# Dealing out the output matmuls of a fused attention and feed-forward kernel in pairs, with the routing of a batch's first pair moved forward in its stretch

## The chip, the cores and the metric

The kernel runs on one core of one Trainium2 chip. The metric is the device time of one execution in microseconds. Every comparison is made with runs of the kernel before on the same chip in the same rounds. "Lost" time below is TensorE's: the length of a stretch less the work in it, counted as instructions times the cadence at which TensorE issues them when nothing waits (the prediction tells where the cadences come from).

## The reference

Clustered attention, then a feed-forward layer with `h * cos(h)` in the middle. There are 4 batches, 8 heads, 768 positions, head size 64; then 3072 tokens, model width 512, inner width 2048.

```
q_assign = argmax(q_n @ c_n.T);  k_assign = argmax(k_n @ c_n.T)       # routing: 16 clusters a head
mask     = q_assign[:, :, :, None] == k_assign[:, :, None, :]
attn     = softmax(where(mask, q @ k.T / 8, -1e9))
x        = (attn @ v) laid out as (tokens, 512)
h        = x @ w_in
out      = (h * cos(h)) @ w_out
```

## The kernel before

Heads are taken two at a time: 16 pairs, four to a batch. The program is a row of **pair stretches**, one per pair, with an **input stage** after the stretches of each batch. A pair stretch has nine score chunks as its main work. Each chunk goes through an exponential on ScalarE:

```
def e_chunk(p, c):
    ps = ps_big.tile([P, CW], FP32, name="big")          # two such PSUM buffers, 1024 columns each
    ...  # 2 or 3 matmuls from the transposed q and k, with the routing as 16 more rows (L332)
    nc.scalar.activation(out=e_flat[...], in_=ps, func=AF.Exp, scale=1.0 / SUNIT)
```

Other work is strewn between the chunks as filling:

```
f_list(p)       # attention times V, 12 times 6 matmuls (L352), then normalization on DVE (L362, L363)
g_list(p)       # transpose of the result into xt: by DMA, or for a batch's last pair by TensorE (L378)
tr_list(p)      # halving of q and k into high and low fp16 parts on DVE (L198, L200), transpose by DMA (L234)
c_list(p)       # routing: 4 times 6 matmuls (L250), then reductions on DVE
ot_list(p)      # transpose of the routing by DMA (L286), four copies of it into qkT (L290)
moe2_list(b, t) # one output tile: 8 items of two matmuls (L416), then a copy on DVE (L421) and a store
```

`merge` spreads a list of filling evenly over the main work by weight. The order on ScalarE and GpSimd is the program's. TensorE, DVE and the DMA queue are put in order by the compiler, which may lift an instruction ahead of its place. At run time an engine takes its instructions in the order it got: in the traces below, DVE stands for 2.50 us and TensorE for 4.15 us at an instruction whose input has not come, with others behind it.

The input stage of a batch is 12 chunks of 16 matmuls (L394), with a cosine on ScalarE (L401) and a product on DVE (L402). A batch has six output tiles. Two are made in its input stage; four are left for the next batch's pair stretches:

```
for s in range(NPE - 1, NPAIR):
    late = s % HPB == 2
    fill = []
    if not late: fill += cs("E", s)              # routing
    fill += trs("E", s)                          # halvings and transposes
    after_s = s > HPB and s % HPB == 1           # the first pair after an input stage
    if not after_s: fill += f_list(s - 1) + g_list(s - 1)
    if m2:                                       # whole output tiles, 16 matmuls each
        left = HPB - (s - 1) % HPB
        keep = 2 if s + HPB >= NPAIR else 0
        for _ in range(-(-max(0, len(m2) - keep) // left)):
            fill += moe2_list(*m2.pop(0))
    if late: fill += cs("E", s)                  # routing of pair s + 2, a batch's first, comes last
    ...
```

In the last stage, TensorE has the last pair's L352, then 12 input chunks, with all the output tiles that are left as filling.

The softmax here doesn't subtract the row's maximum and nothing guards it: scores larger than these inputs give would overflow.

## Time and profile before

The median is 318.27 us of three runs (317.21 to 318.49). The first pairs go another way through the program, and the change doesn't touch them, so the table begins at stretch 5. It is worked out from the timeline of PE.

| part | begins at, us | length, us | lost, us |
|---|---|---|---|
| stretches 5 / 6 / 7 / 8 | 91.40 | 9.28 / 9.65 / 10.91 / 10.24 | 0.57 / 0.27 / 1.38 / 0.38 |
| input stage of batch 1 | 131.48 | 31.70 | 0.44 |
| stretches 9 / 10 / 11 / 12 | 163.18 | 9.34 / 9.65 / 11.34 / 8.19 | 0.63 / 0.27 / 1.81 / 1.73 |
| input stage of batch 2 | 201.70 | 31.85 | 0.65 |
| stretches 13 / 14 | 233.55 | 9.34 / 9.33 | 0.63 / 0.56 |
| stretch 15 and the last stage, to the last tile | 252.22 | 57.41 | 0.21 |

A stretch runs from its first score matmul to the next part's first matmul, so a wait at the head of stretch 8 is counted as lost in stretch 7. Stretch 12 is short since it has no output matmul.

### The profile page before, as it was taken

Reading aid. Unit: us, or ns where it says so; the run is one execution under the profiler, and the core shown is the slowest. Engines: PE = TensorE matmul, PEld = TensorE weight load, DVE = VectorE, ACT = ScalarE, POOL = GpSimd, SP = SyncE. Lnnn points to the kernel's source line nnn. Section 1 sums busy time; section 2 is a strip of 40 time slices with the busy share of each in tenths; the row PEclk is TensorE's granted clock in tenths of the full one; section 3 lists DMA queues with packets and bytes.
Section 4 is the critical chain, followed back from the end, with each engine's and each line's share of the span. In section 5 each row is a group of like instructions: output and inputs, shape, how many; then the busy total and the mean of one; then the engine's idle time right before and its main releaser. Section 6 shows DMA issues by size and latency. Waiting matters only on the chain.

```text
span 316.7 us, 8195 instructions
## 1 busy us (share of the span) xinstructions
PE 305.7 (97%) x3459; PEld 214.8 (68%) x3459; DVE 189.3 (60%) x363; ACT 215.8 (68%) x235; POOL 75.0 (24%) x130
## 2 busy tenths in 40 slices
PE   7999999999999998999999997999999999999995
PEld 2668777887766665688766664787766566766754
DVE  4888887779966245179966145279962114355431
ACT  5688989865469897856569897865479992442220
POOL 2799945120130422220130422220020400000000
PEclk9999999999999999999999999999999999999999
DMA  6579999667597969737596999838482940000012
GB/s 203 201 131 180 234 120 140 165 149 160 88 223 134 147 134 155 195 91 156 83 233 133 145 131 139 205 87 158 94 156 73 74 62 33 35 33 35 33 52 84
DMA packets 87845, 40.25 MB, mean 127 GB/s; under 512 B 76352, under 2 KB 82752, under 8 KB 87808
## 3 DMA queue, kind: packets, MB, share of 16 engines
q1 hardware_dynamic: 57504, 24.19, 34.3%
q0 software_dynamic: 30016, 15.21, 32.4%
q8 instruction: 27, 0.44, 0.6%
q10 hardware_dynamic: 288, 0.33, 0.4%
q14 instruction: 10, 0.08, 0.1%
HBM read 27.30 MB, written 6.29 MB: 106 GB/s over the span
## 4 chain that ended last, share of the span: by engine, by line
PE 83%; ACT 8%; DVE 4%; DMA 4%; issue 1%; SPq 0%; ACTq 0%
PE big L394 25%; PE one L416 22%; PE big L332 17%; PE one L352 10%; ACT e_ring L339 6%; DMA qkT<-ohT 3%; PE one L250 2%; PE one L247 2%; PE one L306 2%; PE one L218 1%; DVE g L402 1%; DMA qk_nat<-in_q_dram 1%; PE one L433 1%; PE one L378 1%; ACT cos_t L401 1%
## 5 line engine op out<-in xcount | busy, mean ns | idle before, releaser
L339 ACT ACTIVATE e_ring<-big 128x1024 f16<-128x1024 f32 x144 | 137.7, 1037 | 16.8 <-PE big L332 15.9
L401 ACT ACTIVATE cos_t<-big,bias_pi 128x1024 f16<-128x1024 f32 x48 | 53.4, 1112 | 68.9 <-PE big L394 68.8
L416 PE MATMUL one<-w_out_sb,g 128*128 128x512 f16 x368 | 93.6, 379 | 0.0
L394 PE MATMUL big<-xt,w_in_sb 128*128 128x256 f16 x768 | 91.4, 273 | 1.0 <-DVE g L402 1.0
L332 PE MATMUL big<-qkT 128*128 128x512 f16 (+1 forms) x384 | 85.4, 325 | 3.7 <-DMA qkT<-ohT 2.6
L394 PEld LDWEIGHTS <-w_in_sb 128*128 128x128 f16 x768 | 74.0, 98 | 16.0 <-DVE g L402 1.8
L402 DVE TENSOR_TENSOR g<-big,cos_t 128x1024 f16<-128x1024 f32 x48 | 58.6, 1222 | 41.4 <-ACT cos_t L401 41.4
L416 PEld LDWEIGHTS <-g 128*128 128x128 f16 x368 | 35.0, 98 | 30.3
L332 PEld LDWEIGHTS <-qkT 128*128 128x128 f16 x384 | 33.3, 97 | 28.2 <-issue 3.7
L352 PEld LDWEIGHTS <-e_ring 128*128 128x128 f16 x1152 | 44.7, 97 | 7.7
L352 PE MATMUL one<-v_ext,e_ring 128*128 128x65 f16 x1152 | 47.2, 193 | 0.0
L421 DVE COPY o_sb<-one 128x512 f32<-128x512 f32 x23 | 15.8, 686 | 30.4 <-PE one L416 30.4
L200 DVE SCALAR_TENSOR_TENSOR stg<-qk_nat,stg 128x384 f16<-128x384 f32 x64 | 33.3, 552 | 0.2
L134 POOL DMA_DIRECT2D v_ext<-in_v_dram x32 | 26.5, 833 | 4.8 <-issue 3.1
L117 POOL COPY pace<-e_ring 1x1 f16<-1x1 f16 x30 | 5.4, 180 | 77.2 <-ACT e_ring L339 77.0
L362 DVE RECIPROCAL recip<-one 128x6 f32<-128x6 f32 x32 | 6.1, 193 | 28.2 <-PE one L352 28.1
L196 POOL TENSOR_SCALAR stg<-qk_nat 128x384 f16<-128x384 f32 x16 | 19.9, 1245 | 8.2 <-DMA qk_nat<-in_q_dram 7.0
L117 POOL COPY pace<-g 1x1 f16<-1x1 f16 x13 | 2.3, 177 | 78.2 <-DVE g L402 63.8
L363 DVE TENSOR_TENSOR av_stage<-one,recip 128x384 f16<-128x384 f32 x32 | 17.7, 557 | 1.0
L194 ACT ACTIVATE stg<-qk_nat 128x384 f16<-128x384 f32 x28 | 13.1, 513 | 2.0 <-DMA qk_nat<-in_q_dram 2.0
L318 DVE TENSOR_SCALAR qkT<-one 16x768 f16<-16x768 f16 (+1 forms) x20 | 10.9, 544 | 3.5 <-PE one L306 2.9
L198 DVE TENSOR_SCALAR stg<-qk_nat 128x384 f16<-128x384 f32 x20 | 6.8, 364 | 8.8 <-DMA qk_nat<-in_q_dram 6.0
(57 smaller groups left out, 168.1 us busy)
## 6 DMA issues: line engine op xcount, KB each, us to landing
out_dram<-o_sb SPq DMA_DIRECT2D x23, 256.0 KB, 2.3
qk_nat<-in_q_dram POOLq DMA_DIRECT2D x10, 384.0 KB, 3.7
qk_nat<-in_k_dram POOLq DMA_DIRECT2D x10, 384.0 KB, 4.1
v_ext<-in_v_dram POOLq DMA_DIRECT2D x32, 96.0 KB, 4.0
w_in_sb<-in_moe_w_in_dram POOLq DMA_DIRECT2D x4, 512.0 KB, 7.1
w_out_sb<-in_moe_w_out_dram POOLq DMA_DIRECT2D x4, 512.0 KB, 6.6
qk_nat<-in_q_dram SPq DMA_DIRECT2D x5, 384.0 KB, 6.5
qk_nat<-in_k_dram SPq DMA_DIRECT2D x5, 384.0 KB, 7.1
```

The source lines that it names most:

```text
L134: nc.gpsimd.dma_start(out=v_bufs[p % NV][:, hh, :, 0:D], in_=v[b, 2 * hp + hh].rearrange("(p t) d -> p t d", p=P))
L196: nc.gpsimd.tensor_scalar_mul(dst[:, :, 0, :], src, ASCALE)
L200: nc.vector.scalar_tensor_tensor(out=dst[:, :, 1, :], in0=src, scalar=ASCALE, in1=dst[:, :, 0, :], op0=ALU.mult, op1=ALU.subtract)
L332: mm = nc.tensor.matmul(ps[:, x:x + n], lhsT=qkT[p, 1, hh][:, jt * P:(jt + 1) * P], rhs=qkT[p, 0, hh][:, col:col + n], start=True, stop=True)
L339: nc.scalar.activation(out=e_flat[:, base + c * CW:base + (c + 1) * CW], in_=ps, func=AF.Exp, scale=1.0 / SUNIT)
L352: nc.tensor.matmul(av[:, i, :], lhsT=e_ring[:, r + j, i * P:(i + 1) * P], rhs=vx[:, j, 0:DE], start=(j == 0), stop=(j == NT - 1))
L363: dve_mark[0] = nc.vector.tensor_tensor(out=av_of[p][:, :, hh, :], in0=av[:, :, 0:D], in1=recip.to_broadcast([P, NT, D]), op=ALU.mult).ins
L394: mm = nc.tensor.matmul(ps[:, fi, :], lhsT=w_in_sb[:, ft, (f0 + fi) * P:(f0 + fi + 1) * P], rhs=xt_of[b][:, ft, cols], start=(ft == 0), st ...
L401: nc.scalar.activation(out=cos_t, in_=ps, func=AF.Sin, bias=bias_pi2, scale=1.0)
L402: dve_mark[0] = nc.vector.tensor_tensor(out=g[:, f0:f0 + FQ, :], in0=ps, in1=cos_t, op=ALU.mult).ins
L416: nc.tensor.matmul(ops, lhsT=g[:, f, i * P:(i + 1) * P], rhs=w_out_sb[:, f, :], start=(f == 0), stop=(f == NFPT - 1))
L421: nc.vector.tensor_copy(out=o_sb, in_=ops)
```

## The change

The intent is that TensorE always has filling. Output tiles are cut into items of two matmuls and dealt out by count. A tile left open by one stretch is closed first thing in the next. Stretch 12 gets a share, and the last stage keeps one tile instead of two. The routing of a batch's first pair moves ahead of the last item of its stretch.

```diff
-        m2 = []
+        m2, m2_items = [], []
+        M2_AT = {1: 10, 2: 7, 3: 8, 0: 7}
+        M2_LAST = {1: 11, 2: 6, 3: 7, 0: 0}
+        m2_done = 0
         for s in range(NPE - 1, NPAIR):
...
+            r = s % HPB
+            n = (M2_LAST if s + HPB > NPAIR else M2_AT)[r]
+            ml, m2_items = m2_items[:n], m2_items[n:]
+            lead = 0
+            if r in (2, 3):
+                lead = -m2_done % (NFPT // 2)
+            m2_done += len(ml)
+            fill = ml[:lead]
+            if r != 2:
                 fill += cs("E", s)
             fill += trs("E", s)
...
-            if late:
+            if r == 2:
                 fill += cs("E", s)
+            fill += ml[lead:]
...
-        rest = moe2_list(*m2.pop(0)) if m2 else []
-        run(rest[:4])
+        rest, m2_items = m2_items[:NFPT // 2], m2_items[NFPT // 2:]
+        run(rest[:2])
         run(fl[NT:])
-        run(rest[4:])
+        run(rest[2:4])
         run(g_list(p))
         for tg in range(NTG):
             fill = []
             if tg == 0:
-                while m2:
-                    fill += moe2_list(*m2.pop(0))
+                fill = rest[4:] + m2_items
```

More of the change, by code (lines that the diff above doesn't have):

```diff
@@ L733, in cs @@
             return r
-        m2 = []
+        m2, m2_items = [], []
+        M2_AT = {1: 10, 2: 7, 3: 8, 0: 7}
+        M2_LAST = {1: 11, 2: 6, 3: 7, 0: 0}
+        m2_done = 0
         for s in range(NPE - 1, NPAIR):
             moe_next = s >= HPB and s % HPB == 0
-            fill = []
-            late = s % HPB == 2
-            if not late:
+            r = s % HPB
[7 more added lines that the diff above has]
+            if r != 2:
                 fill += cs("E", s)
             fill += trs("E", s)
-            after_s = s > HPB and s % HPB == 1
-            if not after_s:
-                fill += f_list(s - 1)
-            if not after_s:
-                fill += g_list(s - 1)
-            if m2:
-                left = HPB - (s - 1) % HPB
-                keep = 2 if s + HPB >= NPAIR else 0
-                for _ in range(-(-max(0, len(m2) - keep) // left)):
-                    fill += moe2_list(*m2.pop(0))
-            if late:
+            if r != 1:
+                fill += f_list(s - 1) + g_list(s - 1)
+            if r == 2:
                 fill += cs("E", s)
+            fill += ml[lead:]
             if s >= NPE:
@@ L776 @@
                 m2 = sorted(m2 + [(b, (NTG - 1) * TPG + i) for i in range(TPG)])
+                m2_items = [it for x in m2 for it in moe2_list(*x)]
+                m2, m2_done = [], 0
         b = B - 1
@@ L790 @@
             if tg == 0:
-                while m2:
-                    fill += moe2_list(*m2.pop(0))
+                fill = rest[4:] + m2_items
             else:
```

## The prediction

> **What bounds the kernel now.** I first read the page's head and the chain that ended last.
>
> ```profile
> PE 305.7 (97%) x3459; PEld 214.8 (68%) x3459; DVE 189.3 (60%) x363; ACT 215.8 (68%) x235; POOL 75.0 (24%) x130
> ...
> PE 83%; ACT 8%; DVE 4%; DMA 4%; issue 1%; SPq 0%; ACTq 0%
> ```
>
> TensorE is the bound, but 97% busy does not mean that 3% is to be had: matmul records overlap. So I took the cadence from the timeline of PE, start of one group to start of the next, where nothing waits: an output matmul (L416, 512 columns) 5.18 us for 24, 0.216 us each; an attention-times-V matmul (L352) 1.09 for 36, 0.030; a routing matmul (L250) 0.60 for 24, 0.025; a score chunk (L332, 1024 columns) 0.433; an input chunk (L394) 1.74. Length of a stretch less count times cadence is what TensorE really lost there.
>
> I cut the timeline at the first score matmul of each pair ("stretch 5" is pair 5). Work: 9 chunks 3.90, a pair's L352 2.18, a pair's routing 0.60, one output tile of 16 matmuls 3.46, six transposes 0.33. Lost, in us: stretches 5 to 8: 0.57, 0.27, 1.38, 0.38 (2.60 together); 9 to 12: 0.63, 0.27, 1.81, 1.73 (4.44); 13 to 15: 0.63, 0.56, 0.12 (1.31); each input stage (32 us long) about 0.5; the last stage, from 261.87, under 0.1. The table by stretch, restricted to L416, for stretches 9, 11, 12, 15 and the start of the last stage (PE busy and its count, weight loads, clock, DMA share, GB/s):
>
> ```profile
> 163.18:172.52 9.34, 4.75 (x17) 1.41 (x16) 1.00 0.87 156
> ...
> 182.17:193.51 11.34, 4.27 (x16) 1.56 (x16) 1.00 0.90 150
> 193.51:201.70 8.19, 0.00 (x0) 0.00 (x0) 1.00 1.06 154
> ...
> 252.22:261.87 9.65, 4.27 (x17) 1.56 (x16) 1.00 0.57 62
> 261.87:278.39 16.52, 7.90 (x33) 2.99 (x32) 1.00 0.09 33
> ```
>
> Weight loads count the output matmuls exactly: 16 in each pair stretch, none in stretch 12, and 32 left for the last stage, which has no idle to put them in. The timeline of PE shows two kinds of loss. First, the wait for routing at the head of stretches 8 and 12:
>
> ```profile
> 119.11 1.03 PE L416 MATMUL one<-w_out_sb,g 128*128 128x512 f16 x4
> 121.24 0.61 PE L332 MATMUL big<-qkT 128*128 128x512 f16 x3 [1.10 <-DMA qkT<-ohT]
> ...
> 190.95 1.03 PE L416 MATMUL one<-w_out_sb,g 128*128 128x512 f16 x4
> 193.51 1.04 PE L332 MATMUL big<-qkT 128*128 128x512 f16 x5 [1.53 <-DMA qkT<-ohT]
> ```
>
> Second, places where PE runs out of filling and goes at ScalarE's pace:
>
> ```profile
> 170.69 0.59 PE L332 MATMUL big<-qkT 128*128 128x512 f16 x2
> 171.12 0.52 PE L352 MATMUL one<-v_ext,e_ring 128*128 128x65 f16 x12
> 171.60 0.59 PE L332 MATMUL big<-qkT 128*128 128x256 f16 x3
> ...
> 199.87 0.59 PE L332 MATMUL big<-qkT 128*128 128x512 f16 x2
> 200.78 0.59 PE L332 MATMUL big<-qkT 128*128 128x256 f16 x3 [0.32 <-ACT e_ring L339]
> ```
>
> From 170.69 to 171.60 is 0.91 us for 0.433 + 12 x 0.030 = 0.80 of work. ScalarE's own pace, from its timeline:
>
> ```profile
> 95.03 12.15 ACT L339 ACTIVATE e_ring<-big 128x1024 f16<-128x1024 f32 x13 [0.35 <-PE big L332]
> ```
>
> That is (12.15 - 1.02) / 12 = 0.93 us an exponential, 8.4 us a stretch. A stretch with over 8.4 us of TensorE work should be bound by TensorE, and one with less leaves TensorE idle.
>
> **What the Trainium skill says.** "Perfetto Trace Analysis", Identifying the Most-Contended Engine, says matmul busy share is a poor measure because of pipelining; the trace agrees: L416 records last 379 ns at a cadence of 216. "TensorE: Matmul & The Clock Gate", Back-to-back issue gap, gives N/2.4 + 2.5 ns, 216 for N = 512, as the isolated gap, which the trace matches; the roughly 131 ns that it gives for sustained streams of that size is not seen here. "DMA: Bandwidth & Descriptors", Issuing engines are not separate DMA queues: all DMAs share 16 engines and interleave. The trace fits: the DMA share is 0.75 to 1.08 in these stretches. "PSUM — Partial Sum Buffer", Specifications: eight banks of 2 KiB per partition. The kernel has all eight allotted, two double ones for chunks and four single ones, so an output tile left open keeps one of four; no line of the profile tells me yet what that costs.
>
> **The change part by part.** An item is two output matmuls, 0.43 us; a tile is eight items.
>
> *Counts.* Items go from 8, 8, 8, 8 to 10, 7, 8, 7 in stretches 5 to 8; from 8, 8, 8, 0 to 10, 7, 8, 7 in 9 to 12; from 8, 8, 8 to 11, 6, 7 in 13 to 15; and from 16 to 8 in the last stage. No matmul is added or removed, so the gain can only be the loss that the moved ones fill.
>
> Work after, in the four stretches: 3.90 + 0.60 + 4.32 = 8.82 (before 7.96, topped up by lifted L352); 3.90 + 2.18 + 0.60 + 3.03 = 9.71; 9.54; 3.90 + 2.18 + 0.33 + 3.03 = 9.44. All exceed ScalarE's 8.4, stretch 12 included (before about 6.5 there). The third and second also begin with the items that close the open tile, so filling is there while the exponentials catch up.
>
> *Routing.* Before, six of the routing matmuls followed chunk 8 and the other 18 chunk 9, with a finished tile's copy in front of the reductions on DVE. By the new weights (673 in all, routing from 532) all 24 come after chunk 8, with one chunk (0.433) and one item (0.433) behind them. That is 0.87 us more ahead of stretch 8. The chain behind it is on the queue's timeline:
>
> ```profile
> 112.64 1.23 SPq L286 DMA_TRANSPOSE ohT<-oh  x1
> 116.75 2.43 SPq L290 DMA_DIRECT2D qkT<-ohT  x4
> ```
>
> Routing matmuls end at 110.3, the transpose is issued at 112.64 (2.3 us of DVE), its result is there at 116.75 (4.1), the four copies are in place by 121.2 (4.5): 10.9 us. After, 0.87 + 9.54 + some 0.15 of gaps = 10.56 stand before it, so 0.3 us of wait remains; since one tile's 256 KB store now lands near the four copies, I take 0.5 to 0.7. The waits shrink by 0.6 and 0.8.
>
> *Sum.* Stretches 5 to 8: I choose remaining losses of 0.2, 0.1, 0.75, 0.3, together 1.35, a gain of 1.25. Stretches 9 to 12: 1.45 remain of 4.44, a gain of 3.0, most of it stretch 12 taking in work that cost full time in the last stage. Stretches 13 to 15: 0.65 of 1.31 remain, a gain of 0.65. Input stages: the list of work in them is unchanged, 0.
>
> *Given back in the last stage.* 16 fewer matmuls are 3.46 us less, but they also covered waits. An input chunk's buffer is reused two chunks later: 1.74 + ScalarE 1.11 + DVE 1.22 + about 0.3 of hand-over, 4.38 from start to start. The timeline has this limit just met:
>
> ```profile
> 274.02 3.66 PE L394 MATMUL big<-xt,w_in_sb 128*128 128x256 f16 x32
> 277.52 1.03 PE L416 MATMUL one<-w_out_sb,g 128*128 128x512 f16 x4
> ```
>
> Chunk 3 starts at 274.02, chunk 5 at 278.39, 4.37 later, with four output matmuls (0.87) between. After, the 16 that are left cover the normalization after the last L352 (about 1.0), the copy of the transposed output (0.5) and chunk 3; then nothing is left for the 0.87 before chunk 5. I take 0.8 lost.
>
> Sum: 1.25 + 3.0 + 0.65 - 0.8 = 4.1 us; 318.27 - 4.1 = 314.2.
>
> **Rivals.** (1) *The wait for routing is fully hidden and the last stage loses nothing*: another 1.3 + 0.8 us, and with every gap in the pair stretches gone the ceiling is 8.35, 309.9. For it: the work per stretch exceeds ScalarE's everywhere. Against it: gaps survive today in stretches with enough work (0.38 in stretch 8). Likely value 312. (2) *The wait stays*: the DMA chain is as long as a stretch, the 16 DMA engines are nearly full, and a store between the transpose and the copies holds the queue in order; TensorE only arrives earlier at the same wait. Then 1.4 of the gain goes: 315.6. (3) *The open tile takes a bank* from the L352 or routing tiles, and TensorE waits for a copy by DVE in new places, perhaps 0.3 in each of six stretches: 316. Against it: DVE was idle for 4.40 us before the copy of a tile in stretches 6 and 10, so it comes at once. (4) *The order of the program is not that of TensorE* (L352 of pair 5 ran inside stretch 5, ahead of its place): the compiler fills gaps by its own lights, and the shares matter little and only stretch 12 and the tail change, about 2 us: 316.3.
>
> **Range and chances.** The middle is 314.2; rival 1 gives the low end, 312.2, rivals 2 to 4 the high end, 316.4. The three runs before differ by 1.3 us. Over 2% needs 311.9, which takes nearly all of rival 1: 0.1. Slower by over 2% has no mechanism in sight: 0.01.
>
> **What would show it.** Right: weight loads of L416 by stretch 20, 14, 16, 14 and 14 in stretch 12; 16 in the last stage before its second group of chunks; the two waits for the routing copies below 0.8 each; a new gap of some 0.8 before the fifth chunk of the last stage, put down to DVE; the lost time of stretches 9 to 12 at about 1.5. Wrong: a wait for routing still over 1 us, new waits of TensorE on DVE in the pair stretches, or ScalarE waiting less while PE's groups stay 0.91 apart.

## The result and the profile after

The kernel after takes 314.32 us (median of 4 runs, 313.56 to 314.81), against 318.27 (317.21 to 318.49). The ratio is 0.988 with a 95% interval of 0.985 to 0.991. Ratios here are the mean time of one kernel's fast runs over that of the other's in the same rounds, so they are not quite the ratio of the medians quoted.

The head of the page looks as before, though the span is 3.7 us shorter; the chain's shares do not:

```profile
PE 303.1 (97%) x3459; PEld 213.8 (68%) x3459; DVE 189.0 (60%) x363; ACT 216.4 (69%) x235; POOL 74.7 (24%) x130
...
PE 84%; DVE 7%; DMA 4%; ACT 1%; issue 1%; SPq 0%; POOL 0%; POOLq 0%; ACTq 0%; DVEq 0%
```

ScalarE's share of the chain fell from 8% to 1%, which fits with TensorE no longer going at its pace. DVE's rose from 4% to 7%, and the load of k (`qk_nat<-in_k_dram`), which was not among the chain's lines that the page lists, now has 4%. The table by stretch restricted to L416 shows that the items went where the change puts them (columns as in the prediction; here stretches 9, 11 and 12):

```profile
162.73:172.07 9.34, 6.04 (x22) 1.89 (x21) 1.00 0.85 145
...
181.62:191.16 9.54, 4.43 (x17) 1.57 (x16) 1.00 0.94 153
191.16:202.29 11.13, 3.84 (x15) 1.33 (x14) 1.00 0.92 151
```

Weight loads are 21, 16 and 14, and stretch 12, which had none, now has 14. The lost time is:

| part | lost before | lost after |
|---|---|---|
| stretches 5 / 6 / 7 / 8 | 0.57 / 0.27 / 1.38 / 0.38 | 0.25 / 0.05 / 0.01 / **2.18** |
| stretches 9 / 10 / 11 / 12 | 0.63 / 0.27 / 1.81 / 1.73 | 0.31 / 0.07 / 0.01 / **1.70** |
| input stages of batches 1 / 2 | 0.44 / 0.65 | 0.44 / 0.44 |
| stretches 13 / 14 | 0.63 / 0.56 | 0.25 / 0.02 |
| stretch 15 and the last stage | 0.21 | 0.43 |

This adds up: 0.11 + 2.35 + 0.21 + 0.92 - 0.22 = 3.37 us gained. Another 0.35 us had been gained already before stretch 5, which begins at 91.06 instead of 91.40. The change doesn't reach there; the repeat runs of the same kernel begin it at 91.51 in one profile, so this is scatter.

The places shown in the prediction answer as follows on the timeline of PE. The wait for the routing at the head of stretch 8 is gone altogether:

```profile
118.99 0.59 PE L416 MATMUL one<-w_out_sb,g 128*128 128x512 f16 x2
119.42 0.60 PE L332 MATMUL big<-qkT 128*128 128x512 f16 x3
```

Two output matmuls start at 118.99, and 0.43 us later, which is their bare cadence, the first score matmul of pair 8 follows without an idle mark. But later in the same stretch there is a wait that the kernel before did not have:

```profile
124.67 0.38 PE L416 MATMUL one<-w_out_sb,g 128*128 128x512 f16 x1
126.58 0.51 PE L378 MATMUL one<-ident,av_stage 128*128 128x128 f16 x6 [1.54 <-DVE av_stage L363]
```

It is 1.54 us in stretch 8 and 1.06 in stretch 12, for the transposes of a batch's last attention result. The profile names DVE's normalization. The timeline of DVE shows what held that up:

```profile
119.46 0.35 DVE L198 TENSOR_SCALAR stg<-qk_nat 128x384 f16<-128x384 f32 x1
122.31 0.42 DVE L198 TENSOR_SCALAR stg<-qk_nat 128x384 f16<-128x384 f32 x1 [2.50 <-DMA qk_nat<-in_k_dram]
...
125.97 0.56 DVE L363 TENSOR_TENSOR av_stage<-one,recip 128x384 f16<-128x384 f32 x1
```

DVE stands idle for 2.50 us at the halving of a k tile that has not landed; the normalizations stand behind it in order. TensorE's own wait is thus for a load, at one remove. In the kernel before, the same k tile was there earlier and stretch 8 began 1.8 us later, so the load cost TensorE nothing:

```profile
120.92 0.63 DVE L198 TENSOR_SCALAR stg<-qk_nat 128x384 f16<-128x384 f32 x2 [1.09 <-DMA qk_nat<-in_k_dram]
```

The new wait thus has two parts: the stretch comes 1.8 us earlier, and the load, though issued 0.2 us earlier, lands 1.4 us later. Why it lands later was not tested.

Last, the queue's and GpSimd's timelines for the routing's transfers, which answer to those shown before:

```profile
111.33 1.22 SPq L286 DMA_TRANSPOSE ohT<-oh  x1
114.10 2.43 SPq L290 DMA_DIRECT2D qkT<-ohT  x4
```

```profile
114.39 0.71 POOL L128 DMA_DIRECT2D qk_nat<-in_q_dram  x1 [0.32 <-issue]
```

The transpose is issued 1.3 us earlier, and its result is there after 2.77 us instead of 4.11. It is now done before the load of q is issued at 114.39. In the kernel before, that load was issued at 114.64, in the middle of the transpose.

### The profile page after: what moved, and what is told of

It is laid out like the page before. It is cut to its first block, busy times and chain, and to the rows that moved or that the text cites. A ratio compares the mean times of both kernels' runs of the same rounds, so it can differ in the third digit from the quotient of the medians.

```text
span 313.0 us, 8197 instructions
## 1 busy us (share of the span) xinstructions
PE 303.1 (97%) x3459; PEld 213.8 (68%) x3459; DVE 189.0 (60%) x363; ACT 216.4 (69%) x235; POOL 74.7 (24%) x130
## 4 chain that ended last, share of the span: by engine, by line
PE 84%; DVE 7%; DMA 4%; ACT 1%; issue 1%; SPq 0%; POOL 0%; POOLq 0%; ACTq 0%; DVEq 0%
PE big L394 25%; PE one L416 24%; PE big L332 17%; PE one L352 8%; DMA qk_nat<-in_k_dram 4%; PE one L250 2%; PE one L247 2%; PE one L306 2%; DVE g L402 2%; DVE stg L200 2%; PE one L218 1%; DVE av_stage L363 1%; PE one L433 1%; DMA cn_raw<-in_centroids_dram 1%; PE one L378 1%
## 5 line engine op out<-in xcount | busy, mean ns | idle before, releaser
L416 PE MATMUL one<-w_out_sb,g 128*128 128x512 f16 x368 | 95.7, 379 | 0.0
L416 PEld LDWEIGHTS <-g 128*128 128x128 f16 x368 | 35.0, 98 | 28.0
L352 PEld LDWEIGHTS <-e_ring 128*128 128x128 f16 x1152 | 43.1, 97 | 7.0
L352 PE MATMUL one<-v_ext,e_ring 128*128 128x65 f16 x1152 | 45.2, 193 | 0.0
L258 DVE TENSOR_REDUCE csum<-one 128x192 f32<-128x384 f32 x22 | 11.2, 549 | 0.0
```

What stands on the lines that cost most here:

```text
L352: nc.tensor.matmul(av[:, i, :], lhsT=e_ring[:, r + j, i * P:(i + 1) * P], rhs=vx[:, j, 0:DE], start=(j == 0), stop=(j == NT - 1))
L416: nc.tensor.matmul(ops, lhsT=g[:, f, i * P:(i + 1) * P], rhs=w_out_sb[:, f, :], start=(f == 0), stop=(f == NFPT - 1))
```

## The experiments

All outputs are right. My theory after reading the result had three parts. **A**: filling stretch 12 and dealing by items gives the gain. **B**: the routing's wait went, but its place was taken by a wait for the load of k, through DVE's order. **C**: how long the routing's transfers take depends on whether they meet the load of q. The rivals were that the new wait has another cause (the open tile's PSUM bank, or late L352 matmuls), that only stretch 12 counts, and that shares do or don't matter.

### The changed kernel again

> The changed kernel unaltered, as the reference on this chip for the three runs beside it. Expected 314.3 us against 318.3 before, ratio 0.988.

It took 315.08 us (314.95 to 315.58), with 318.35 for the kernel before on this chip; the ratio is 0.990. The waits for the normalization are there again, 1.78 and 0.96.

### Loads earlier, no order changed

```diff
-                    l_at("E", 4 * b + 3, 3, 4 * b + 5)
+                    l_at("E", 4 * b + 3, 0, 4 * b + 5)
```

> Changed kernel, but the loads of q and k of pairs 9 and 13 are issued at chunks 0 and 2 of stretches 7 and 11 instead of 3 and 5; the order of every engine is the same. Theory: the 1.54 and 1.06 us that TensorE waits for the normalization at the end of stretches 8 and 12 come from DVE, which stands in order behind the halving of a k tile that has not landed (2.50 and 2.07 us idle). Landed some 3 us earlier, the wait goes: up to 2.9 us less (1.69 and 1.22 lost there), if nothing else is touched. But the transpose of the routing, issued at 111.33, then collides with this load as it did in the kernel before (4.1 us instead of 2.8), so I expect it to come back to over 4 us, with a wait for the routing copies of 0 to 0.6 at the head of stretches 8 and 12: 312.0 to 313.0. Rival: the wait is caused by the open output tile's bank or by the later L352; then the time stays at 314.3 and the wait for the normalization too.

It took 312.66 us (312.09 to 312.84), ratio 0.982, against 315.08 on the same chip. The order of instructions is the same on every engine; only the loads of q and k start some 3 us earlier. The wait for the normalization is gone from both stretches, so the cause is the lateness of the load. And the other half of the expectation came too. GpSimd's timeline, the queue's and PE's:

```profile
111.51 0.71 POOL L128 DMA_DIRECT2D qk_nat<-in_q_dram  x1 [0.32 <-issue]
```

```profile
111.56 1.22 SPq L286 DMA_TRANSPOSE ohT<-oh  x1
116.58 3.81 SPq L290 DMA_DIRECT2D qkT<-ohT  x4
```

```profile
120.61 0.61 PE L332 MATMUL big<-qkT 128*128 128x512 f16 x3 [0.81 <-DMA qkT<-ohT]
```

The transpose of the routing and the load start together, and the transpose takes 5.0 us instead of 2.8 (4.7 for pair 12). A wait of 0.81 for the routing is back in stretch 8. With the loads of q and k moved and nothing else, this shows part C: loads beside it lengthen the transpose. That the 4.1 us in the kernel before, where the load of q came 2.0 us behind, have the same cause is read from this and not tested.

### Halvings after the normalizations

```diff
-            fill += trs("E", s)
+            if r:
+                fill += trs("E", s)
             if r != 1:
                 fill += f_list(s - 1) + g_list(s - 1)
+            if r == 0:
+                fill += trs("E", s)
```

> Changed kernel, but in stretches 8 and 12 the halvings of the next pair's q and k stand after the normalizations in the program, and so on DVE. Theory: the normalization no longer waits for the load, the 1.69 and 1.22 us lost before the transposes go, and with them most of the 0.36 before them: 311.2 (310.8 to 311.9), clearly under the changed kernel. Rival (the bank or the L352 are late): 314.3, wait unchanged.

It took 311.68 us (311.45 to 311.89), ratio 0.979 (interval 0.977 to 0.981), 3.4 us less than the changed kernel on the same chip. This is the version that beats both. On the timeline of PE the transposes follow at once:

```profile
124.55 0.38 PE L416 MATMUL one<-w_out_sb,g 128*128 128x512 f16 x1
124.76 0.50 PE L378 MATMUL one<-ident,av_stage 128*128 128x128 f16 x6
```

Stretches 8 and 12 lose 0.37 each. They lost 2.42 and 1.60 in the profile of the changed kernel on this chip. The difference, 3.28, is nearly all of the 3.4. Here no load was moved: it was DVE's order that passed a DMA's lateness on to TensorE. The run with earlier loads had left the open tile's bank and the order of the L352 as they were, so those rivals fall.

### The same, with the routing at its old place

The edit is to put `fill += ml[lead:]` ahead of the routing in stretches 6 and 10; only the order on TensorE differs from the last run.

> As the run with the later halvings, but the routing matmuls of pairs 8 and 12 stand behind the last item of their stretch, where the kernel before had them (six after chunk 8, 18 after chunk 9); only the order on TensorE differs. Theory: the last routing matmul is 0.87 us later, the transpose is then issued about 112.2 and meets the load of q, so takes about 4 us, and the copies land 1.5 to 2 us later, which leaves waits of 0.5 to 1.2 at the head of stretches 8 and 12: 1.0 to 2.4 us slower than the run with the later halvings alone, 312.2 to 313.6. Rival: the place of the routing is of no account, the waits went because TensorE has more to do before: same time as that run within 0.3 us.

It took 312.25 us (median of six runs; five of them 311.78 to 312.92). That is half a microsecond more than without the routing at its old place, and I expected 1.0 to 2.4. No wait for the routing came back: the transpose was issued at 112.17 and took 2.6 us all the same. In this profile, then, the routing goes out early enough even at its old place; below, the changed kernel with the routing there has the wait in one profile and not in another.

The sixth run, the profiled one, took 316.13. It shows what the later halvings risk. The transposed q and k of pair 9 landed late, and the routing of that pair (L250) waited for them in the input stage:

```profile
143.45 0.79 PE L250 MATMUL one<-cside,qkT 128*128 128x32 f16 x24 [2.72 <-DMA qkT<-stg]
```

That input stage took 36.20 us instead of 31.70. Only 2.72 of the 4.5 us are the wait; over the 3.5 us from 143.40 on, the granted clock is 0.58, which accounts for another 1.5 (estimated as 3.5 x 0.42). The transpose is issued at 128.83 in the version with later halvings, and at 122.51 in the kernel before, while its result is wanted at 140.56 and 142.84. The margin fell from 20 to 12 us.

### Stretch 12 filled, and nothing else

```diff
-                keep = 2 if s + HPB >= NPAIR else 0
+                keep = 1 if s + HPB > NPAIR else 0
```

> Kernel before, with only the count changed: stretch 12 takes the whole fourth tile, and the last stage keeps one tile instead of two. Theory: stretch 12 lost 1.73 us beside its wait, and takes 3.46 us of work for some 2.0 more; the last stage gives back 3.46 less about 0.3: 316.8 (316.3 to 317.3), with the waits for the routing copies still 1.1 and 1.5. Rival (all of the gain comes from this tile): 314.3.

It took 318.21 us (316.72 to 318.89), ratio 1.000: no gain, where I expected 1.5 us and the rival 4. In stretch 12 it went as expected: the stretch is 2.06 us longer (10.25 for 8.19) and holds 3.46 of work that was in the last stage. But the last stage gave back only 1.64 us (55.77 for 57.41, from stretch 15 on), since the single tile that it has left is spent before the first input chunk, eight and eight matmuls as the old program has it:

```profile
274.13 3.65 PE L394 MATMUL big<-xt,w_in_sb 128*128 128x256 f16 x32 [1.11 <-DVE g L402]
```

Stretch 15 and the last stage lose 2.03 us in it, against 0.43 in the changed kernel. The changed kernel deals out its last tile as 4, 4 and 8 matmuls; I put the 1.6 us down to that, though no run has that change alone.

### The routing ahead of its stretch's whole tile, and nothing else

In the kernel before, the two lines that add the routing late are moved ahead of the output tile.

> Kernel before, with only the routing of pairs 8 and 12 moved ahead of that stretch's output tile. It is then issued some 4 us earlier, and the waits of 1.10 and 1.53 at the head of stretches 8 and 12 go. Theory: most of that is swallowed in stretch 8, where the normalization then waits for the halvings behind the late load of k (the changed kernel gained only 0.1 us from stretch 5 to stretch 8), while stretch 12 has no filling to lose: 317.3 (316.7 to 317.9). Rival: the waits were lost time in full, 315.6.

The six runs scatter: 316.45 and 318.25 at a mean granted clock of 1.000 and 0.999, 320.32 and 320.37 at 0.994 and 0.993, and two slow (over 1.5% above the fastest run of the same kernel), 321.25 and 321.96. The four fast runs give a ratio of 1.003 (0.998 to 1.007), no gain. The waits for the routing's copies are gone in the profile, and there is a new one before the routing (a slow run). The timeline of PE, and the table of windows over the next 3.4 us (busy time and count of PE, PEld, which is TensorE's weight loads, DVE, ACT and POOL, then the granted clock):

```profile
174.57 0.34 PE L352 MATMUL one<-v_ext,e_ring 128*128 128x65 f16 x6
179.07 0.50 PE L250 MATMUL one<-cside,qkT 128*128 128x32 f16 x12 [4.15 <-DMA qkT<-stg]
```

```profile
179.00:182.40 3.40, 3.33 (x32) 1.83 (x33) 2.11 (x5) 1.73 (x2) 0.00 (x0) 0.51 0.67 159
```

The routing of pair 12 needs that pair's transposed q and k, which land at 179; placed ahead of the tile it is due at 174.9, and TensorE, which takes its instructions in order, stands for 4.15 us. For the next 3.4 us its clock is granted at half. The Trainium skill tells of this: "TensorE: Matmul & The Clock Gate", Part 1, The HAM clock gate, says that a monitor halves the clock after an idle window of 3413 ns. The trace agrees on the halving: 0.51 over the 3.4 us after the stall, and 1.00 before and after. It does not agree that a whole window has to be idle: the wait of 2.72 us in the fourth run (the later halvings with the routing at its old place) was enough as well. The waits of up to 1.78 us, in the repeat of the changed kernel, were not.

One such spell takes about 0.005 off the mean clock of a run (half of 3.4 us in 319), so the two fast runs at 0.994 and 0.993 probably had the stall and the two at full clock not; those two average 317.35, which is what I expected. Two runs don't prove it.

So the routing has an earliest place. In this run it could not start before 179; the changed kernel starts it at 180.15, and nothing waits there.

### Even shares, first try

The counts of the changed kernel are set to 8, 8, 8, 8.

> Changed kernel, but eight items in every pair stretch (8, 8, 8, 8 and 8, 8, 8 at the end) instead of 10, 7, 8, 7 and 11, 6, 7; everything else stays. Theory: the first two of each four again run at ScalarE's pace, about 0.5 us lost in stretches 5 and 6, 9 and 10, and 13 and 14; in the first two cases the wait for the normalization, which is set by a load, swallows part of it: 315.0 (314.6 to 315.8). Rival: only the total moved into stretch 12 counts, 314.3.

This run failed as a test. With whole tiles, no items are left to close at the head of a stretch, so the routing came ahead of the whole tile, with the same stall as in the last run (3.69 us). Runs were 315.23 to 319.91 fast and 320.48 to 321.69 slow, the ratio 0.999 (0.994 to 1.005). One thing can be read from it: stretches 5, 9, 13 and 14 lost 0.57, 0.63, 0.63 and 0.56, to the hundredth what the kernel before loses, and not 0.25, 0.31, 0.25 and 0.02.

### The changed kernel with the routing at its old place, twice

The edit is that of the fourth run ("The same, with the routing at its old place"), made to the changed kernel.

> Changed kernel, but the routing matmuls of pairs 8 and 12 stand behind the last item of their stretch, as in the kernel before; only the order on TensorE differs. Theory: a wait for the routing copies of 0.5 to 1.2 comes back at the head of stretches 8 and 12, but the wait for the normalization at the end of the same stretches becomes shorter by as much, since that one ends when the load of k has landed: 314.3 to 314.8. Rival: both waits add up, 315.5 to 316.5.

It took 313.56 us (313.30 to 313.71), ratio 0.986, and was not slower than the changed kernel at all. To have both on one chip they were run again:

> The changed kernel once more, so that the next three runs have it on the same chip: 314.3 to 315.1, ratio to before 0.988 to 0.990.

> The changed kernel with the routing of pairs 8 and 12 behind the last item again, now beside the changed kernel on one chip. On another chip it gave 313.56. Theory: the earlier place of the routing is worth nothing in the changed kernel, since the transpose of the routing finishes before the load of q begins in either case by now, and its copies, when they go earlier, lie beside the load of q and k and make k land later, which the normalization waits for: 0.5 to 1.5 us faster than the changed kernel. Rival: the first run was luck of the chip; same time within 0.3, or slower by the 0.4 that it lost beside the later halvings.

The changed kernel took 313.94 to 314.75 in five runs (median of all six 314.22); a sixth, the profiled one, took 1734.60 us. TensorE itself was slow in it: busy for 1728.0 us, with 1713 ns for the record of an output matmul where 379 is usual, while an exponential on ScalarE took 1024 ns as ever. Its page has no row for the granted clock. It was left out; I don't know its cause. The routing at its old place took 314.00 (313.52 to 314.55). The ratios are 0.9875 and 0.9871, which is the same; my 0.5 to 1.5 us did not show. The two profiles of this kernel tell why the place is worth so little. In the second, stretch 8 began with a wait of 0.92 for the routing, and had no wait for the normalization. In the first it was the other way: none for the routing, and 0.72 for the normalization. When TensorE waits at the head, it comes later by as much, and by then k has landed. The two waits stand in for one another. The transpose took 2.6 us in both profiles; what differed is the copies behind it, of which the second landed 4.2 us after the first was issued in the one and 5.7 in the other.

### Even shares, with the routing where the change has it

```diff
-        M2_AT = {1: 10, 2: 7, 3: 8, 0: 7}
-        M2_LAST = {1: 11, 2: 6, 3: 7, 0: 0}
+        M2_AT = {1: 8, 2: 8, 3: 8, 0: 8}
+        M2_LAST = {1: 8, 2: 8, 3: 8, 0: 0}
...
-                lead = -m2_done % (NFPT // 2)
+                lead = 7
```

> Changed kernel with eight items in every pair stretch, and this time with seven items of the tile ahead in the third and fourth stretch of each batch, so that the routing stands where the change has it, ahead of one item (in the earlier try with even shares it fell ahead of the whole tile, and TensorE waited 3.69 us for the transposed q and k of pair 12). Theory: stretches 5, 9 and 13 lose 0.6 each instead of 0.27, and 14 loses 0.5 instead of 0.02; in the first two batches the wait for the normalization takes up part of it: 0.9 to 1.6 us slower than the changed kernel, 315.3 to 316.4. Rival: only the total moved into stretch 12 counts, within 0.3.

It took 313.66 us (312.98 to 314.32), ratio 0.9855 (0.983 to 0.988), beside 0.9875 (0.986 to 0.989). I expected it slower by about 1.2; it is not slower. The test is less clean than its title. By the new weights only 18 of the 24 routing matmuls come after chunk 8 and six after chunk 9, so the transpose is issued 2.2 us into stretch 7 instead of 1.5; waits for the routing of 1.21 and 0.59 are back, and those for the normalization are gone. By the two runs just above, that exchange costs nothing that can be measured. The table by window restricted to L416 shows why, here for stretch 5:

```profile
91.22:100.50 9.28, 6.04 (x22) 1.89 (x21) 1.00 0.88 154
```

The program gives stretch 5 sixteen output matmuls, and TensorE runs 21 there, as with the shares of the change. The compiler lifts the opening items of the next stretch into the gap. In the first try, where a stretch opened with L352, it lifted L352, which then has to keep ScalarE's pace. So it is the items at the head of the next stretch that fill stretches 5, 9 and 13, and not the counts. Stretch 14 alone lost some: 0.21 instead of 0.02, where I had expected 0.5.

### Later halvings, and one item held for the input stage

To the version with later halvings, `M2_AT[0]` is set to 6, and the item left over stands at the end of the first group of input chunks.

> The run with the later halvings (311.7), with one more change: one item of stretches 8 and 12 is held back and stands at the end of the first group of chunks of the input stage that follows, where TensorE waits 0.44 us for the product on DVE. Theory: the two gaps of 0.44 shrink to 0.1, and stretches 8 and 12 keep 9.0 us of work, over the 8.4 of ScalarE: 311.0 (310.6 to 311.5). Rival: the gap moves behind the item, 311.7. In either case a single run with the transposed q and k of pair 9 late, as one of ten had, would be some 4 us longer.

It took 312.36 us (311.45 to 313.40), ratio 0.9815, so nothing was gained over 311.68 on the other chip. In the profile, batch 2's stage lost 0.28 instead of 0.44, but batch 1's lost 1.20, of which 0.75 was the wait for pair 9's transposed q and k, the same as in the 316.13 us run. An earlier end of stretch 8 eats into the same 12 us of margin.

## Why the prediction was right or wrong

The total was right, 314.32 for 314.2, but several of its terms were wrong in opposite ways, so that its closeness is partly luck. By the table the terms come to 3.37 and not 4.1, and 0.35 of the profiles' difference is scatter ahead of stretch 5.

**What bounds the kernel** was right. No work was removed and the gain is lost time filled. The DMA share of 0.75 to 1.08 that I gave holds for stretches 5 to 12 only; stretches 13 to 15 had 0.57 to 0.68.

**The counts** were right (21, 13, 16 and 14 weight loads for 20, 14, 16 and 14; 14 in stretch 12), but the reason that I gave, that work per stretch beats ScalarE's 8.4 us, was too simple. Even shares did as well. What was right in rival 4 is that the compiler's order, and not the program's count, fills the first stretches of each batch. Where rival 4 failed is its sum: it had stretch 12 and the tail as all that changes, and stretch 12 alone is worth nothing unless the tail is dealt out too.

**Stretches 13 to 15** were put at 0.65 and gave 0.92 from 13 and 14. **Stretches 9 to 12** were put at 3.0 and gave 2.35. **The last stage** was put at a loss of 0.8 and lost 0.22 more than before. The gap before the fifth input chunk, which I put at 0.8, is 0.2: the 16 matmuls that are left are indeed spent on earlier waits (4, 4, 2 and 6 by 270.95), but the compiler lifted three of the next output tile into the gap. The timeline of PE:

```profile
270.95 3.66 PE L394 MATMUL big<-xt,w_in_sb 128*128 128x256 f16 x32
274.45 0.81 PE L416 MATMUL one<-w_out_sb,g 128*128 128x512 f16 x3
275.33 1.91 PE L394 MATMUL big<-xt,w_in_sb 128*128 128x256 f16 x16
```

**The routing** is the step that failed: "0.3 us of wait remains; since one tile's 256 KB store now lands near the four copies, I take 0.5 to 0.7". None remained. The routing did leave 0.86 us earlier in its stretch, as predicted (the transpose is issued 1.45 us into stretch 7 instead of 2.31), and from there the first two copies took the same 4.5 us; the mis-sized term is the transpose. I had taken its 4.1 us as its own duration, and it took 2.8 when it was ahead of the load of q. That the other 1.3 us were the load beside it is what the run with earlier loads makes likely.

**Stretches 5 to 8** failed with it: "I choose remaining losses of 0.2, 0.1, 0.75, 0.3, together 1.35, a gain of 1.25". They were 0.25, 0.05, 0.01 and 2.18, a gain of 0.11. The wait for the routing did not shrink but was exchanged for a wait for the normalization, behind a load. Of my rivals, the third had TensorE waiting for DVE in new places, but for a PSUM bank, which is not the cause; none had the load. The prediction named new waits on DVE as a sign that it is wrong, and in this part it is.

What stands is a gain from filling that no single edit shows: stretch 12 alone gave nothing, the routing's place nothing, the counts nothing. That the items at the heads of the stretches and the tail dealt out give it is read from the table by stretch; no run has either alone.

The place of the routing in the change gains nothing that can be measured in the changed kernel (0.9875 and 0.9871). Once the halvings are out of the way the two medians differ by 0.6 us (311.68 and 312.25), less than the scatter of the kernel before, so a worth there is not shown either.

What stays open: the reason for the 1734.6 us run, why the load of k lands later in the changed kernel, and how often the version with later halvings meets the late transpose. It was not seen in its own four runs, once in six of the version that differs only on TensorE, and in part in the last version's profile.

## What to carry to other kernels

When a wait goes, look for what its length was hiding: follow the other inputs of the stretch that now begins earlier, and above all the loads that stand ahead of something urgent in an engine's fixed order. Put work that depends on a load behind work that doesn't, as late as its own consumer allows, and check that consumer's margin in several runs. A transfer's duration in a trace is that of its company; before adding it into a chain, see what else was in flight.

## What the Trainium skill lacked or had wrong

- "TensorE: Matmul & The Clock Gate", Back-to-back issue gap: it gives about 131 ns per matmul for a sustained stream at N = 512. Here a stream of 24 such matmuls with their weight loads keeps a cadence of 216 ns, which is the page's figure for an isolated gap.
- "DMA: Bandwidth & Descriptors", DMA Transpose (X-bar): it has no figure for a small transpose beside other traffic. Here the routing's transpose (its input is 128 x 768 elements of fp16) had its result ready 2.6 to 3.4 us after issue where the 384 KB load of q was issued 2.2 us after it or later, 3.6 to 4.2 where that was 2.0 us, and 4.7 to 5.0 where both were issued together. Other traffic counts too: in the two runs that sent pair 8's transpose out right behind another one, it took 3.8 with that load 7 us away, and over all pairs and runs it ran from 2.5 to 8.6 (the run of 1734.6 us left out).
- "TensorE: Matmul & The Clock Gate", Part 1, The HAM clock gate: it gives one idle window of about 3.4 us as what brings the half clock. Here a wait of 2.72 us brought it too, like those of 3.69 and 4.15; waits of up to 1.78 us in the pair stretches did not.
- "Perfetto Trace Analysis", Identifying Dependency Chains: it says to look at the semaphores that an instruction waits on. That leads to DVE's normalization for the 1.54 us wait here, and not to the load; the page does not say to look, on the engine named, at what stands ahead in its order (2.50 us idle for a k tile).
